# Conversion transfers on GpSimd's queue and fills from SBUF on SyncE's queue, in a fused attention, MoE and MLP kernel

## The chip, the cores and the metric

One of the cores of a Trainium2 chip runs the whole kernel. The metric is the device time of one execution in microseconds (us), the median of several runs. The engines are TensorE (PE in the profile), VectorE (DVE), ScalarE (ACT), GpSimd (POOL) and SyncE (SP), each with an instruction queue of its own; a DMA is issued by an instruction in such a queue and waits in it, in order, like any other.

## The reference

Three layers stand one behind the other; the output of each is the input of the next.

```python
# q, k, v: [4, 12, 448, 64]
scores = scale * np.matmul(q, k.transpose(0, 1, 3, 2))
scores = np.einsum('bhij,hg->bgij', scores, w_pre)      # heads mixed
scores = scores - np.max(scores, axis=-1, keepdims=True)
attn = np.exp(scores)
attn = attn / (np.sum(attn, axis=-1, keepdims=True) + 1e-09)
attn = np.einsum('bhij,hg->bgij', attn, w_post)         # heads mixed again
x = np.matmul(attn, v)                                  # -> 1792 tokens x 768
...
# mixture of 8 experts, the best one for each token
expert_idx = np.argmax(x @ w_gate, axis=1)
out[mask] = gate_w[mask, None] * (np.maximum(xe @ w1[e], 0.0) @ w2[e])
...
# MLP, 768 -> 2048 -> 768
h = x @ w_in
out = (h * np.cos(h)) @ w_out
```

All inputs are float32 but w_in and w_out of the MLP, which come as float64.

## The kernel before, in words

**The stages.** The attention runs from the start to about 490 us, the experts to about 795 us, the MLP to the end. The change lies in the attention and in what runs beside it.

**The attention** takes 16 chunks of a batch's query rows. For each chunk `score` (L292) multiplies heads with heads into S tiles in SBUF. A chunk falls into blocks of ten query rows (180 in all). `block(n)` (L520) handles one of them: `relay` (L309) has a DMA on SyncE copy ten rows x 12 heads of S, 210 KB, into an x tile of 120 partitions (6 of these tiles rotate); an m matmul (L527) mixes the heads; VectorE takes the maximum `nm` (L530); ScalarE the exponential `E` (L534); VectorE the sum's reciprocal `rs` (L537, L539) and the scaled mixing matrix `kr` (L542); the pa matmuls (L548) mix again and transpose; a copy (L551) puts the result into `AT`. An m and the four pa of a block show in the trace as 2 and 8 records. The heads of the next batch are loaded on SyncE as kn and qn (L200) and vn (L209) and transposed on TensorE (L222). The first batch's heads come as fk and fq (L251), which GpSimd copies into kn and qn (L262) and late (L270). When a chunk is done, the products with v (L355, L366, L414) give rows of tokens: `rows_out` (L417) collects a chunk's rows in the tile xr (one buffer) and stores them to `xs` in DRAM (L426).

**The fills.** Eleven stretches of 64 rows in `ys` (the DRAM buffer that the experts write and the MLP reads) are padding that no expert may write, and they need some finite contents. `fill[X]` (L1865) writes one of them behind each of the first eleven xs stores, from 64 of the rows that were just stored.

**The conversion** (`narrow64`, L1765) turns w_in and w_out into float32 copies `wi` and `wo` in DRAM that the MLP loads later. There are 64 pieces of 128 x 384 numbers. `piece` (L651) is a loop body of five steps: load 128 x 3072 bytes, 384 KB, into a tile W of 2 buffers (L1786); square on ACT (L1790, into sq); three bit operations on VectorE (L1796 to L1798, into a tile f of 2 buffers); store f, 192 KB (L1802).

**What sets the order.** `Plan` (L63) runs a list schedule when the kernel is built: each step of a task has an engine, a cost in us (and kilobytes for a transfer) and a rank; the earliest possible step is taken next, and the engine's queue gets instructions in that order. `dma(d)` is a cost on SyncE. The pieces run as background (`bg=True`): a step of theirs is put where it delays no step in front. So costs, and the engine that they stand on, change the order of every queue, and the order is fixed before the kernel runs.

**The hand-over.** `between` (L1807) starts the experts: the row gather `gather(0)` (L1269, an indirect DMA on GpSimd into xg), its transposes px on TensorE (L1277), and expert weights r loaded on SyncE (L1251, L1255).

Of the kernel before, what the change touches and what calls it, by code (L numbers as in the profile page):

```python
# [12 lines left out]
F32 = mybir.dt.float32  # L13
# [166 lines left out]
def attention(ctx, qctx, tc, q, k, v, w_pre, w_post, wg, xs, lg, ident, nb=4, side=None, route=None, fill=()):  # L180
# [3 lines left out]
    nc = tc.nc  # L184
# [179 lines left out]
    def moved(copy, out, in_, n):  # L364
        if copy:
            copy(out, in_)  # L366
        else:
            bal.copy(out, in_, n)
# [48 lines left out]
    def rows_out(X, half, pt, copy=None):  # L417
        b, c = chunks[X]
        i0, n, _ = CH[c]
        t0 = b * S + i0  # L420
        if half == 0:
            XRW[X] = wk.tile([120, 768], F32, tag="xr", name=f"xr{X}", bufs=1)
        xr = XRW[X]
        moved(copy, xr[:n, half * 384 : half * 384 + 384], pt[:n].rearrange("p a d -> p (a d)"), 384)
        if half == 1:
            nc.sync.dma_start(out=xs[t0 : t0 + n], in_=xr[:n])  # L426
            if X < len(fill):
                fill[X](xs[t0 : t0 + HR])

    def rows(X):  # L430
        for half in range(2):
            rows_out(X, half, rows_mm(X, half))
# [35 lines left out]
    with tc.manual_schedule(engines=START):  # L468
        spin(9)
        for j in range(H // 2 + 1):  # L470
# [20 lines left out]
            if j > 0:  # L491
                n = CH[0][1]
# [13 lines left out]
    def dve(d):  # L506
        return {"DVE": (d - 0.07, d)}

    def act(d):
        return {"ACT": (d - 0.07, d)}  # L510
# [4 lines left out]
    def dma(d):  # L515
        return {"SP": (d, d)}
# [76 lines left out]
    def products(X):  # L593
        n = CH[chunks[X][1]][1]
        b = chunks[X][0]
        ats = [("AT", k) for k in range(first_of[X], end_of[X] + 1)]
        px = []
        for half in range(2):
            yield dict(run=pe(0.02 * n + 0.02), tiling="col", onward=True, on=ats + [("V", b)], take=["q"] + (["xc"] if half == 0 else []), give=["AT"] if half else [], ends=[("av", X, half)])
            px.append(av_mm(X, half))  # L600
        for half in range(2):
            eng = yield dict(run=copying(3 * n), give=["q"], ends=[("xc", X)] if half else [])
            av_out(X, half, px[half], by[eng])
        for half in range(2):
            yield dict(run=pe(0.33), take=["q"] + (["xr"] if half == 0 else []))
            pt = rows_mm(X, half)
            eng = yield dict(run=copying(384), give=["q"])
            rows_out(X, half, pt, by[eng])

        yield dict(run={"none": (0.0, 3.0)}, give=["xr"])  # L610
# [38 lines left out]
        yield dict(run={"none": (0.0, 0.0)}, on=[("xcs", G_[-1])], give=["xc"])  # L649

    def piece(i, load, square, bits, store):  # L651
        yield dict(run=dma(0.58), kb=393, take=["W"])
        load(i)
        yield dict(run=act(0.56), take=["sq"])
        square(i)
        for d, op in zip((0.36, 0.56, 0.56), bits(i)):
            yield dict(run=dve(d), take=["f"] if d == 0.36 else [], give=["W", "sq"] if False else [])
            op()
        yield dict(run=dma(0.42), kb=197, give=["W", "sq"])
        store(i)  # L660
        yield dict(run={"none": (0.0, 0.0)}, give=["f"])

# [29 lines left out]
    if side is not None:  # L692
        count, *ops = side
        for i in range(count):
            plan.add(4 + i * 170 / count, piece(i, *ops), bg=True)
    with tc.manual_schedule(engines=START | {mybir.EngineType.SP}):
        plan.run()
    return SimpleNamespace(
        last=last, X=len(chunks) - 1, av_mm=av_mm, av_out=av_out, logits_mm=logits_mm, logits_out=logits_out, logit_tiles=logit_tiles,
        rows_mm=rows_mm, rows_out=rows_out, pq=pq,  # L700
    )

# [6 lines left out]
HR = 64  # L709
# [477 lines left out]
class Experts:  # L1187
# [69 lines left out]
    def load(self, s, anew=False):  # L1257

        for i in range(3):
            self.load1(s, i, anew)  # L1260
        for i in range(4):
            self.load2(s, i, anew)
# [502 lines left out]
def narrow64(ctx, tc, pairs):  # L1765

    nc = tc.nc
    V = nc.vector
    wk = ctx.enter_context(tc.tile_pool(name="f64", bufs=2))
    C = 384
    jobs = []
    for src, dst in pairs:
        n = src.shape[0] * src.shape[1] // P
        sv = src.bitcast(I32).rearrange("(p a) d -> p (a d)", p=P)
        dv = dst.rearrange("(p a) d -> p (a d)", p=P)
        for j in range(n // C):  # L1780
            jobs.append((sv[:, 2 * C * j : 2 * C * j + 2 * C], dv[:, C * j : C * j + C]))
    W, SQ, F = {}, {}, {}

    def load(i):
        W[i] = wk.tile([P, C, 2], I32, tag="W", name=f"W{i}")
        nc.sync.dma_start(out=W[i], in_=jobs[i][0].rearrange("p (n two) -> p n two", two=2))  # L1786

    def square(i):
        SQ[i] = wk.tile([P, C], F32, tag="sq", name=f"sq{i}")
        nc.scalar.activation(SQ[i], W[i][:, :, 1].bitcast(F32), AF.Copy, scale=2.0**-112)  # L1790

    def bits(i):
        w, sq = W.pop(i), SQ.pop(i)
        f = F[i] = wk.tile([P, C], I32, tag="f", name=f"f{i}")
        return (
            lambda: V.tensor_scalar(f, w[:, :, 0], 29, None, op0=ALU.logical_shift_right),  # L1796
            lambda: V.scalar_tensor_tensor(f, sq.bitcast(I32), 3, f, op0=ALU.logical_shift_left, op1=ALU.bitwise_or),
            lambda: V.scalar_tensor_tensor(f, w[:, :, 1], -0x80000000, f, op0=ALU.bitwise_and, op1=ALU.bitwise_or),  # L1798
        )

    def store(i):
        nc.sync.dma_start(out=jobs[i][1], in_=F.pop(i).bitcast(F32))  # L1802

    return len(jobs), load, square, bits, store


# [41 lines left out]
def kernel(ctx, tc, q, k, v, w_pre, w_post, w_gate, w1, w2, w_in, w_out, out):  # L1848
    nc = tc.nc
    glob = ctx.enter_context(tc.tile_pool(name="glob", bufs=1))  # L1850
    dram = ctx.enter_context(tc.tile_pool(name="dram", bufs=1, space=bass.MemoryType.DRAM))
    ys = dram.tile([NH * HR + NF * P, 768], F32, name="ys")
    xs = dram.tile([NT * P, 768], F32, name="xs")
# [8 lines left out]
    ro = Routing(cr, tc, glob, consts, lg)  # L1862
    fill = []
    for at in (*range(HSURE * HR, NH * HR, HR), *range(NH * HR + NSURE * P, NH * HR + NF * P, HR)):
        fill.append(lambda a, at=at: nc.gpsimd.dma_start(out=ys[at : at + HR], in_=a))  # L1865
    with ExitStack() as cm:
        with ExitStack() as c:
            with ExitStack() as cq:
# [129 lines left out]
```

## Time and profile before

| | us |
|---|---|
| median of 3 runs | 1283.37 (1282.93 to 1285.02) |
| profiled execution, its own time | 1286.4 |
| span of its records | 1284.6 |
| TensorE busy in the span | 1265.5 (99%) |
| VectorE busy | 987.1 (77%) |
| ScalarE busy | 755.4 (59%) |
| GpSimd busy | 88.5 (7%) |

The span runs from the first to the last record of one execution. Busy times leave out register, semaphore and DMA-issuing instructions. An engine with a share of 99% over the whole span is read best by its waits: how many there are, and what ended each. In a timeline, an x behind a row is the number of records merged into it, and the bracket is the time in which the engine stood idle ahead of it, with the instruction that released it. A queue's own rows (SPq for SyncE) give the time that an issue took.

### The profile page before, as it was taken

The numbers are of one execution on the slowest core, as the hardware profiler recorded it, in microseconds if no ns is written. First come the engines' busy times: TensorE is split into PE (matmuls) and PEld (weight loads), VectorE is DVE, ScalarE is ACT, GpSimd is POOL, SyncE is SP. The second block draws the span as 40 slices with busy tenths as digits, with TensorE's granted clock in tenths as the row PEclk, the third lists the DMA queues.
The fourth block names the chain that finished last, engine by engine and source line by source line (L and its number), as shares of the span: only waits on it lengthen the run. The fifth ranks groups of instructions, "written<-read, shape, count | busy, mean of one in ns | idle before, by whom it ended". The sixth has DMA issues, their size and how long they took to land.

```text
span 1284.6 us, 24332 instructions
## 1 busy us (share of the span) xinstructions
PE 1265.5 (99%) x8719; PEld 1026.9 (80%) x8719; DVE 987.1 (77%) x2382; ACT 755.4 (59%) x1422; POOL 88.5 (7%) x97
## 2 busy tenths in 40 slices
PE   9999999999999999999999999999999999999997
PEld 5777777777877787876667998898888888888886
DVE  7888888888878878986667998987666667766663
ACT  6566666666666656766667988665434434444432
POOL 3000000000000000210000110011000200001001
PEclk9999999999999999999999999999999999999999
DMA  7768757775766546599977944664333333234201
GB/s 201 229 201 216 246 195 220 220 241 181 219 224 220 181 157 237 215 358 343 379 261 263 358 147 159 198 207 162 98 124 123 128 118 120 78 104 139 77 26 52
DMA packets 149008, 244.90 MB, mean 191 GB/s; under 512 B 42240, under 2 KB 106176, under 8 KB 148704
## 3 DMA queue, kind: packets, MB, share of 16 engines
q1 hardware_dynamic: 142528, 217.90, 51.7%
q0 software_dynamic: 3936, 19.27, 4.6%
q10 hardware_dynamic: 2416, 6.10, 1.2%
q8 instruction: 71, 1.16, 0.4%
q14 instruction: 57, 0.47, 0.1%
HBM read 219.05 MB, written 31.85 MB: 195 GB/s over the span
## 4 chain that ended last, share of the span: by engine, by line
PE 57%; DMA 1%; ACT 0%; DVE 0%; issue 0%; POOLq 0%; POOL 0%; ACTq 0%
PE op L1667 18%; PE dh L1727 18%; PE yp L1471 8%; PE h L1355 6%; PE yp L1426 2%; PE h L1406 2%; PE ph L1454 1%; PE dpt L1590 1%; PE px L1277 1%; DMA xg<-xs,idh 1%; PE ph L1415 0%; PE px L1388 0%; DVE wl L1169 0%; ACT wh L1168 0%; POOLq L1952 0%
## 5 line engine op out<-in xcount | busy, mean ns | idle before, releaser
L548 PEld LDWEIGHTS pa<-kr,E 120*112 120x112 f32 (+1 forms) x1440 | 166.5, 177 | 46.2 <-issue 32.7
L1169 DVE TENSOR_TENSOR wl<-r,wh 128x768 fp32r<-128x768 f32 (+1 forms) x176 | 180.5, 1062 | 23.1 <-ACT wh L1168 21.7
L548 PE MATMUL pa<-kr,E 120*112 120x120 f32 (+1 forms) x1440 | 181.5, 269 | 2.1 <-DVE rs L537 1.0
L1168 ACT CAST wh<-r 128x768 fp32r<-128x768 f32 (+1 forms) x176 | 160.9, 928 | 34.3 <-PE h L1355 19.3
L527 PE MATMUL m<-x,kpre 120*120 120x448 f32 x360 | 159.1, 546 | 2.2 <-DMA x<-S 2.2
L1169 DVE TENSOR_TENSOR wil<-wi,wih 128x768 fp32r<-128x768 f32 x64 | 60.8, 953 | 129.9 <-ACT wih L1168 129.9
L1667 PE MATMUL op<-woh,gh 128*128 128x512 f32 x448 | 151.9, 339 | 0.9 <-ACT gh L1698 0.9
L1667 PE MATMUL op<-wol,gh 128*128 128x512 f32 x448 | 150.9, 337 | 0.0
L1667 PE MATMUL op<-woh,gl 128*128 128x512 f32 x448 | 150.4, 336 | 0.0
L1168 ACT CAST wih<-wi 128x768 fp32r<-128x768 f32 x64 | 53.6, 843 | 155.9 <-PE dh L1727 155.9
L534 ACT ACTIVATE E<-m,nm 120x448 f32<-120x448 f32 x180 | 114.3, 635 | 46.6 <-DVE nm L530 21.5
L530 DVE TENSOR_REDUCE nm<-m 120x1 f32<-120x448 f32 x180 | 111.0, 617 | 20.4 <-PE m L527 16.7
L1727 PE MATMUL dh<-dxh,wih 128*128 128x512 f32 (+1 forms) x384 | 109.7, 365 | 0.3 <-ACT dhs L1731 0.3
L1727 PE MATMUL dh<-dxl,wih 128*128 128x512 f32 (+1 forms) x384 | 109.0, 363 | 0.0
L1727 PE MATMUL dh<-dxh,wil 128*128 128x512 f32 (+1 forms) x384 | 108.3, 363 | 0.0
L1667 PEld LDWEIGHTS op<-woh,gh 128*128 128x128 f32 x448 | 84.9, 189 | 11.4 <-ACT gh L1698 1.1
L1667 PEld LDWEIGHTS op<-wol,gh 128*128 128x128 f32 x448 | 84.9, 190 | 9.8
L1667 PEld LDWEIGHTS op<-woh,gl 128*128 128x128 f32 x448 | 84.7, 189 | 9.2
L551 ACT COPY AT<-pa 112x480 f32<-112x480 f32 (+1 forms) x103 | 58.4, 567 | 45.6 <-PE pa L548 40.0
L1168 ACT CAST woh<-wo 128x768 fp32r<-128x768 f32 x64 | 53.2, 836 | 53.0 <-PE op L1667 52.3
L355 PEld LDWEIGHTS px<-AT,vn 112*64 112x64 f32 x1536 | 73.7, 137 | 8.1 <-issue 3.2
L1727 PEld LDWEIGHTS dh<-dxl,wih 128*128 128x128 f32 x384 | 69.3, 189 | 11.5
(350 smaller groups left out, 2448.7 us busy)
## 6 DMA issues: line engine op xcount, KB each, us to landing
r<-in_moe_w_dram SPq DMA_DIRECT2D x39, 1024.0 KB
r<-in_moe_w_dram SPq DMA_DIRECT2D x52, 768.0 KB
x<-S SPq DMA_DIRECT2D x172, 210.0 KB
wi<-wi SPq DMA_DIRECT2D x32, 768.0 KB
wo<-wo SPq DMA_DIRECT2D x32, 768.0 KB
p<-in_moe_w_dram SPq DMA_DIRECT2D x15, 1024.0 KB
p<-in_moe_w_dram SPq DMA_DIRECT2D x20, 768.0 KB
W<-in_moe_w_in_dram SPq DMA_DIRECT2D x32, 384.0 KB
```

The source lines that it names most:

```text
L355: nc.tensor.matmul(px[64 * e : 64 * e + 64, pr, :n], VN[b, g // 3][:, g % 3, cc], AT[X][:, cc, g, :n], start=(cc == 0), stop=(cc == 3))
L527: nc.tensor.matmul(ps[:M, :S], kpre[:M, :M], x[:M], start=True, stop=True)
L530: nc.vector.reduce_max(nm[:M], ps[:M, :S], axis=AX.X, negate=True)
L534: last["act"] = nc.scalar.activation(e[:M], ps[:M, :S], AF.Exp, bias=nm[:M], scale=1.0, accum_out=sg[:M])
L548: nc.tensor.matmul(pa[:112, c, :120], e[:M, c * 112 : c * 112 + 112], kr[:M], start=True, stop=True)
L551: last["post"] = by[eng](AT[X][:, :, :, j0 : j0 + m], pa[:112, :, :120].rearrange("p c (g i) -> p c g i", i=10)[:, :, :, :m])
L1168: self.latest["A"] = nc.scalar.copy(hi, src).ins
L1169: self.latest["V"] = nc.vector.tensor_tensor(lo, src, hi.bitcast(F32), op=ALU.subtract).ins
L1355: self.nc.tensor.matmul(hp[n], a[:, k], w[:, n * 512 : n * 512 + 512], start=(k == 0 and i == 0), stop=(k == 5 and i == 2))
L1471: self.nc.tensor.matmul(yp[n][:, :384], a[:, k], w[:, n * 384 : n * 384 + 384], start=(k == 0 and i == 0), stop=(k == 7 and i == 2))
L1667: nc.tensor.matmul(bank[:, to], g[:, u * P : u * P + P], w[:, of], start=first, stop=(f == 15 and i == 2), skip_group_check=(n == 1))
L1727: nc.tensor.matmul(hp[:, :N], w[:, k], x[:, k, :N], start=(k == 0 and i == 0), stop=(k == 5 and i == 2))
```

## The change

The conversion's loads (L1786) and stores (L1802) are issued on GpSimd in place of SyncE, and the planner counts 1.0 us of GpSimd for each in place of 0.58 and 0.42 us of SyncE. The fills (L1865) are issued on SyncE in place of GpSimd, and their source is 64 rows of xr in SBUF rather than the 64 rows of xs in DRAM, so they read what the store ahead of them reads and don't wait for it.

```diff
@@ rows_out
             nc.sync.dma_start(out=xs[t0 : t0 + n], in_=xr[:n])
             if X < len(fill):
-                fill[X](xs[t0 : t0 + HR])
+                fill[X](xr[:HR])
@@ piece
-        yield dict(run=dma(0.58), kb=393, take=["W"])
+        yield dict(run={"POOL": (1.0, 1.0)}, kb=393, take=["W"])
         load(i)
...
-        yield dict(run=dma(0.42), kb=197, give=["W", "sq"])
+        yield dict(run={"POOL": (1.0, 1.0)}, kb=197, give=["W", "sq"])
         store(i)
@@ narrow64
-        nc.sync.dma_start(out=W[i], in_=jobs[i][0].rearrange("p (n two) -> p n two", two=2))
+        nc.gpsimd.dma_start(out=W[i], in_=jobs[i][0].rearrange("p (n two) -> p n two", two=2))
...
-        nc.sync.dma_start(out=jobs[i][1], in_=F.pop(i).bitcast(F32))
+        nc.gpsimd.dma_start(out=jobs[i][1], in_=F.pop(i).bitcast(F32))
@@ the main kernel
-        fill.append(lambda a, at=at: nc.gpsimd.dma_start(out=ys[at : at + HR], in_=a))
+        fill.append(lambda a, at=at: nc.sync.dma_start(out=ys[at : at + HR], in_=a))
```

SyncE's queue has 1137 instructions before and 1020 with the change (128 leave, 11 come), GpSimd's 130 and 257. What stands in the queues at three places is shown below; a row is the line, the operation, what it writes and what it reads, with the program's buffer numbers.

SyncE in the first blocks of the attention, where x are the operands of the m matmuls, kn and qn the next batch's heads, W a piece's load; before:

```order
L309 DMA x6_561<-S0_275 120x1x448
L209 DMA vn0_2_569<-in_v_dram 112x3x256
L309 DMA x7_577<-S0_275 120x1x448
L200 DMA qn1_0_589<-in_q_dram 112x4x64 x2
L1786 DMA W0_607<-in_moe2_w_in_dram 128x768
L309 DMA x8_616<-S0_275 120x1x448
L309 DMA x9_628<-S0_275 120x1x448
L209 DMA vn0_3_641<-in_v_dram 112x3x256
L309 DMA x10_646<-S0_275 120x1x448
L309 DMA x11_663<-S0_275 120x1x448
L1786 DMA W1_672<-in_moe2_w_in_dram 128x768
L309 DMA x12_680<-S1_482 120x1x448
```

and with the change:

```order
L200 DMA qn1_0_563<-in_q_dram 112x4x64 x2
L309 DMA x6_578<-S0_275 120x1x448
L200 DMA kn1_1_585<-in_k_dram 112x4x64 x2
L209 DMA vn0_2_602<-in_v_dram 112x3x256
L309 DMA x7_611<-S0_275 120x1x448
L309 DMA x8_627<-S0_275 120x1x448
L309 DMA x9_643<-S0_275 120x1x448
L309 DMA x10_654<-S0_275 120x1x448
L309 DMA x11_672<-S0_275 120x1x448
L200 DMA qn1_1_677<-in_q_dram 112x4x64 x2
L209 DMA vn0_3_701<-in_v_dram 112x3x256
L309 DMA x12_708<-S1_486 120x1x448
```

W0 and W1 have left the queue, x7 to x11 stand closer together, and heads have taken some of the room.

GpSimd in the start, among the copies of the first batch's heads, before:

```order
L262 COPY kn0_2_297<-fk_193 112x2x4x64
L262 COPY qn0_2_299<-fq_194 112x2x2x64
L929 MEMSET edge_7630 128x56
L262 COPY kn0_3_327<-fk_193 112x2x4x64
L262 COPY qn0_3_329<-fq_194 112x2x2x64
L262 COPY kn0_4_357<-fk_193 112x2x4x64
```

and with the change:

```order
L262 COPY kn0_2_297<-fk_193 112x2x4x64
L262 COPY qn0_2_299<-fq_194 112x2x2x64
L1786 DMA W0_478<-in_moe2_w_in_dram 128x768
L1786 DMA W1_482<-in_moe2_w_in_dram 128x768
L262 COPY kn0_3_327<-fk_193 112x2x4x64
L262 COPY qn0_3_329<-fq_194 112x2x2x64
L929 MEMSET edge_7630 128x56
L262 COPY kn0_4_357<-fk_193 112x2x4x64
```

W0 and W1 stand between the copies of the third and of the fourth pair of heads. At the end of the attention GpSimd's queue has W63's load, the stores of f62 and f63, and then xg0, the first gather (L1269); before, eleven fills and nothing of the conversion stood ahead of xg0.

TensorE in the start, where s1_8 to s1_11 are scores of the second chunk and m0 the first block; before:

```order
L292 MATMUL s1_6_513<-KH0_3_347,QL0_3_352 120x448
L292 MATMUL s1_7_514<-KH0_3_347,QL0_3_352 120x448
L527 MATMUL m0_527<-x0_478,kpre_211 120x448
L527 MATMUL m1_536<-x1_480,kpre_211 120x448
L292 MATMUL s1_8_540<-KH0_4_380,QH0_4_384 120x448
L292 MATMUL s1_9_541<-KH0_4_380,QH0_4_384 120x448
L292 MATMUL s1_8_540<-KL0_4_381,QH0_4_384 120x448
```

and with the change:

```order
L292 MATMUL s1_10_541<-KH0_5_410,QH0_5_414 120x448
L292 MATMUL s1_11_542<-KH0_5_410,QH0_5_414 120x448
L292 MATMUL s1_10_541<-KL0_5_411,QH0_5_414 120x448
L292 MATMUL s1_11_542<-KL0_5_411,QH0_5_414 120x448
L292 MATMUL s1_10_541<-KH0_5_410,QL0_5_415 120x448
L292 MATMUL s1_11_542<-KH0_5_410,QL0_5_415 120x448
L527 MATMUL m0_557<-x0_480,kpre_211 120x448
L527 MATMUL m1_572<-x1_484,kpre_211 120x448
L527 MATMUL m2_581<-x2_503,kpre_211 120x448
L527 MATMUL m3_590<-x3_505,kpre_211 120x448
L527 MATMUL m4_600<-x4_525,kpre_211 120x448
L548 MATMUL pa0_614<-kr0_598,E0_574 112x120 x4
```

Before, m0 and m1 stand ahead of the twelve score matmuls of s1_8 to s1_11; with the change these twelve stand ahead of m0, and m0 to m4 follow each other.

## Rows read from the trace of the kernel before

**Rows 1.** Engines by stage: us, busy of PE, PEld, DVE, ACT, POOL; clock, DMA, GB/s
```profile
24.00:490.00 466.00, 461.55 (x4215) 355.36 (x4215) 391.41 (x1321) 288.77 (x709) 6.51 (x12) 1.00 0.68 210
...
10.00:12.00 2.00, 2.00 (x19) 1.38 (x19) 1.17 (x3) 1.78 (x5) 0.51 (x1) 1.00 1.22 224
```

**Rows 2.** TensorE's timeline in the first blocks: start us, us, engine, line, operation [idle before]
```profile
21.03 0.98 PE L527 MATMUL m<-x,kpre 120*120 120x448 f32 x2
23.28 0.98 PE L527 MATMUL m<-x,kpre 120*120 120x448 f32 x2 [1.27 <-DMA x<-S]
...
31.91 0.98 PE L548 MATMUL pa<-kr,E 120*112 120x120 f32 x8
32.73 0.92 PE L527 MATMUL m<-x,kpre 120*120 120x448 f32 x2
33.48 0.98 PE L548 MATMUL pa<-kr,E 120*112 120x120 f32 x8
35.41 0.98 PE L527 MATMUL m<-x,kpre 120*120 120x448 f32 x2 [0.94 <-DMA x<-S]
```

**Rows 3.** TensorE's timeline at its four later waits
```profile
106.42 0.38 PE L222 MATMUL tp<-ident,qn 112*128 112x112 f32 x2 [1.08 <-DMA qn<-in_q_dram]
...
134.40 0.33 PE L548 MATMUL pa<-kr,E 108*112 108x120 f32 x1 [0.62 <-ACT E L534]
...
249.75 0.43 PE L548 MATMUL pa<-kr,E 120*112 120x120 f32 x2 [0.96 <-DVE rs L537]
...
354.05 0.57 PE L222 MATMUL tp<-ident,kn 112*128 112x112 f32 x4 [0.29 <-DMA kn<-in_k_dram]
```

**Rows 4.** SyncE's queue in the timeline: issues at 33, 98 and 128 us
```profile
33.35 0.52 SPq L1786 DMA_DIRECT2D W<-in_moe_w_in_dram  x1
...
98.01 0.57 SPq L1786 DMA_DIRECT2D W<-in_moe_w_in_dram  x1
...
99.63 1.27 SPq L200 DMA_DIRECT2D qn<-in_q_dram  x2
...
127.92 0.42 SPq L1786 DMA_DIRECT2D W<-in_moe_w_in_dram  x1
```

**Rows 5.** Who waited for whom, whole span: total us, times, longest us
```profile
ACT sq L1790 <- DMA W<-in_moe_w_in_dram: 22.2, 14, 4.9
...
SPq L1802 <- DVE f L1798: 36.8, 24, 4.1
```

**Rows 6.** ScalarE's timeline at one of its waits for a W
```profile
133.10 0.56 ACT L1790 ACTIVATE sq<-W 128x384 f32<-128x384 f32 x1 [1.58 <-DMA W<-in_moe_w_in_dram]
```

**Rows 7.** Two lines' DMAs on GpSimd: issue ns min/median/max; us to landing min/median/max
```profile
L1865 POOL DMA_DIRECT2D ys<-xs x11: 486/486/539, 65.3 to 374.6; - x11
...
DMA to landing us min/median/max: 3.1/4.3/6.2
...
L1269 POOL DMA_INDIRECT xg<-xs,ids x13: 944/955/1914, 452.5 to 728.4; - x13
...
DMA to landing us min/median/max: 3.8/6.9/14.3
```

**Rows 8.** GpSimd's timeline at three places, and VectorE's beside the last
```profile
7.62 0.40 POOL L262 COPY qn<-fq 112x256 f32<-112x256 f32 x1
...
12.45 0.40 POOL L262 COPY qn<-fq 112x256 f32<-112x256 f32 x1 [0.35 <-DMA fq<-in_q_dram]
...
539.24 9.67 POOL L1269 DMA_INDIRECT xg<-xs,idh  x1 [6.91 <-PE px L1388]
...
541.98 6.16 DVE L1169 TENSOR_TENSOR wl<-r,wh 128x768 fp32r<-128x768 f32 x7
```

**Rows 9.** The end of the attention: TensorE's first px, VectorE's nm before the last conversion operation
```profile
490.52 0.71 PE L1277 MATMUL px<-ident,xg 128*128 128x128 f32 x5
...
481.31 0.62 DVE L530 TENSOR_REDUCE nm<-m 120x1 f32<-120x448 f32 x1
```

## Prediction

> **What bounds the kernel now.** I read four views, in this order: engines by stage, TensorE's timeline at the start, who waited for whom, and the timelines of the two queues that the change touches. The stage that holds nearly all of the change is the attention, 24 to 490 us. There TensorE is busy 461.55 of 466.00 us at a granted clock of 1.00, while VectorE has 391.41, ScalarE 288.77 and GpSimd 6.51 us [rows 1]. So the stage ends when TensorE has got through its list, and only two things can move the time: TensorE's few waits, and work that is added to its list (none is). The stages behind it run in an unchanged order and are not touched, apart from the hand-over at 490 us.
>
> TensorE's waits are small and can be counted. In the start, the second m (L527) waits for its x tile: it starts at 23.28, the first at 21.03 [rows 2]. An m that has its operand gives way to its successor after 0.75 us (32.73 to 33.48), though it is drawn 0.92 to 0.98 long; so the true wait there is 23.28 - 21.03 - 0.75 = 1.50 us, where the bracket says 1.27. Likewise a pa (L548) takes 0.82 us start to start (31.91 to 32.73) and is drawn 0.98: each bracket is about 0.16 short. After 24 us there are five waits worth naming: 0.94 at 35.41 for an x tile [rows 2], and 1.08, 0.62, 0.96 and 0.29 at 106.42, 134.40, 249.75 and 354.05 [rows 3]. Together 3.89 us by the brackets, 3.89 + 5 x 0.16 = 4.7 us true.
>
> What they have in common is SyncE's queue. At 33.35 it issues a conversion load W for 0.52 us, and only behind it the x tiles that the m at 35.41 and its successors want; at 98.01 another W (0.57 us) stands ahead of the q heads issued at 99.63 that TensorE awaits until 106.42 [rows 4]. The queue also stood 36.8 us in 24 waits for f (L1802), with x tiles and heads queued behind [rows 5]. The waits at 134.40 and 249.75 come by ScalarE: it sits 1.58 us at 133.10 for a W [rows 6] that was issued at 127.92 [rows 4], then the exponential comes late.
>
> **The change part by part.** *Taken off SyncE:* 64 loads and 64 stores, with their 36.8 us of waiting. The x tiles and heads then go out earlier; the five waits become 0 at best. Bounds 0 to -4.7; I take -4.7, since an issue that stands ahead is 0.5 us or more and the waits are of that size.
>
> *Put on GpSimd:* 128 issues. The trace has no plain load of this size on that queue. The nearest rows are the fills (L1865), 0.486 to 0.539 us, and the row gathers (L1269), median 0.955 us [rows 7]: 128 x 0.49 = 63 to 128 x 0.955 = 122 us, on an engine with 6.51 us of work in the stage's 466. That is 13 to 26% of it: hidden, 0 us. Its cover is that one piece comes every 450 / 64 = 7.0 us and needs two issues. A store that waits for f now holds up the next loads on GpSimd instead, but the next load but one needs the same tile W to come free, by the same L1798, so little is lost.
>
> *Waits that may appear.* Before, ScalarE waited 14 times for a W (22.2 us) [rows 5] and two of these reached TensorE. The loads' way to landing may be no shorter from GpSimd (fills land in a median of 4.3 us [rows 7]). I take one new wait of the mean size, 3.89 / 5 = 0.78, rounded to +0.7; bounds 0 and +3.9 (as many new as old).
>
> *Order on TensorE at the start.* Before, m0 and m1 run, then twelve score matmuls, then m2; now the twelve run ahead of m0. They take the place in which TensorE waited for x1, since x1 lands by 23.28 while the list is busy: -1.5 us (all but none of the 1.50). The five m that follow in a row are 0.75 us apart, which the x tiles, one issue each, about follow.
>
> *Two loads at the start.* W0 and W1 now stand on GpSimd behind the copy at 7.62 [rows 8] and wait for nothing, so 2 x 384 KB go out from 8 us on, when first heads are still on their way: at 10 to 12 us the DMA share is 1.22 at 224 GB/s [rows 1]. 786 KB at 224 GB/s is 3.5 us; bounds 0 (they fill gaps) to +3.5 (all of it reaches TensorE). I take the middle, +1.8: the queues share the engines, so at most about half of their time should go to the new loads, and GpSimd's copy of the heads at 12.45 [rows 8] already waits for its data, so that such a delay shows. The two issues also push back GpSimd's own copies by 1 to 1.9 us.
>
> *The fills:* 11 move to SyncE, 0.49 us each there, read SBUF and need no wait for the xs store. 11 x 0.5 = 5.4 us on a queue that lost 128 issues; 0 us. On GpSimd they would have to wait up to 48.8 us for the store ahead of them with conversions queued behind, so this part is a condition of the first and brings nothing alone.
>
> *The first gather.* L1269 now stands behind the last two stores of the conversion. The last L1798 comes just behind the nm that now runs at 481.31 [rows 9], so f63 is ready at 482.5, its store is issued by 483.5, the gather by 484.6. It landed in 3.8 to 6.9 us (minimum and median [rows 7]): 488.4 to 491.5, and TensorE wants it at 490.52 [rows 9]. So 0 to +1.0, with a slow issue (1.914 in place of 0.955) to +1.9; I take +0.4.
>
> Sum: -4.7 - 1.5 + 1.8 + 0.7 + 0.4 = -3.3 us. The profiled execution lasted 1286.4 us (span 1284.6), the median of the runs is 1283.37; it lies 3.0 above them and is not one of the three, so the difference is applied to both: 1283.37 - 3.3 = **1280.1 us** (profiled: 1283.1).
>
> **The rivals.** *Nothing is lost anywhere:* no start shift, no new wait, no late gather: -6.2, 1277.2 us. For it: the DMA engines' share is 0.68 in the stage [rows 1].
>
> *The gain is eaten at both ends:* start shift at its bound and the gather late by 1.5: -4.7 - 1.5 + 3.5 + 0.7 + 1.5 = -0.5, 1282.9 us. For it: the share of 1.22 at 10 us; against: the early heads were issued before the W.
>
> *The waits only move:* the x tiles and heads land no earlier, because their transfers, not their issue, are late. Then the term of -4.7 is 0 and that for new waits too: -1.5 + 1.8 + 0.4 = +0.7, 1284.1 us. For it: the q heads of 99.63 landed 6.8 us later, and at most 0.6 of this was the W's issue [rows 4]. The Trainium skill speaks for this rival ("DMA: Bandwidth & Descriptors", Issuing engines are not separate DMA queues): transfers started by any engine run on the same 16 DMA engines, and spreading them saves only issue time. By that rule alone the gain is no more than the issue time that stands in front of a late tile, about 0.5 us each or 2.5 in all, which would give 1282.3; no run here tests it yet.
>
> *Slower: GpSimd's issues are held up by VectorE.* One gather issue took 9.67 us at 539.24, in the middle of back-to-back L1169 operations on VectorE (seven of them, 6.16 us, from 541.98 [rows 8]), against a median of 0.955 [rows 7]. VectorE is 84% busy in the attention. If issues stretch beyond 3.5 us on the mean, two of them no longer fit into a piece's 7.0 us, W comes late, and each late W costs TensorE 0.78 + 0.16 us as at 134.40 and 249.75; every fifth of 64 is 13 x 0.94 = +12.2, less the 3.3: 1292.3 us. Against it: the 11 fills, spread over the same attention with the same VectorE work, all took 0.486 to 0.539 us [rows 7]. The Trainium skill has the rule behind such a case ("SBUF — State Buffer", SBUF: two separate sides): GpSimd writes the descriptors of its DMAs itself and cannot while VectorE runs an operation in a two-port mode. The fills' rows don't show it in this stage; the gather's row does look like it.
>
> **How the numbers follow.** Chances: the forecast 0.48; nothing lost 0.14; eaten at both ends 0.18; the waits only move 0.12; GpSimd held up 0.08. What a measurement of this kernel can tell from no change is 0.2%, 2.6 us: faster is below 1280.8, slower above 1285.9. Of the forecast's 0.48 I count 0.36 as faster and 0.12 as same; with 0.14 that is 0.50 faster. Same: 0.12 + 0.16 + 0.10 = 0.38. Slower: 0.08 + 0.02 + 0.02 = 0.12. The range goes from 1276.7 (nothing lost, less half a microsecond, as low as a run shown lies under the median) to 1284.6 (the waits only move, plus the same); left out are the last rival and the tails, 0.2.
>
> **What would show it.** Right: on TensorE in 24 to 490 us less than 1.5 us of waits in brackets, no wait for x at the second m, L1786 on GpSimd at 0.5 to 1.1 us each, and the stage's end, the first px (L1277), 3 to 4 us ahead of 490.52. Start contention: heads' copies on GpSimd later than 12.45 by over a microsecond, and the first m later than 22.4. The gather: a wait for xg ahead of L1277. GpSimd held up: L1786 and L1802 issues of several microseconds beside VectorE's work, and ScalarE's waits for W above 22.2 us. I am wrong if TensorE has lost its waits and the span has not become shorter: then its list has grown elsewhere, by order alone.

## The result, and the profile after

The changed kernel is slower. Its median is 1294.17 us against 1283.15 us for the kernel before in the same set of runs: a ratio of 1.008, with a 95% interval of 1.0067 to 1.0092, so +11 us where -3.3 was forecast. In a second set of runs (a1_again, below) it is 1295.85 us, ratio 1.0085 (1.0065 to 1.0105). The changed kernel's eight runs in the two sets go from 1291.3 to 1298.2 us, the 21 of the kernel before in the second set from 1281.5 to 1288.2: they don't overlap.

Where does it go? The page of the changed kernel gives TensorE nearly the same busy time as before, 1265.9 us, in a span that is 5.5 us longer (its profiled execution, 1291.8 us, is one of its fastest); GpSimd has 152.8 us.

```profile
span 1290.1 us, 24392 instructions
...
PE 1265.9 (98%) x8719; PEld 1026.2 (80%) x8719; DVE 985.3 (76%) x2379; ACT 756.8 (59%) x1425; POOL 152.8 (12%) x214
```

So the list is not longer; TensorE waits more. The waits of TensorE in 24 to 500 us, changed kernel (waiter, what it waited for: total us, times, longest us):

```profile
PE m L527 <- DMA x<-S: 6.8, 6, 2.8
PE tp L222 <- DMA qn<-in_q_dram: 2.0, 3, 1.2
PE tp L222 <- DMA kn<-in_k_dram: 0.9, 1, 0.9
```

Before, the same three stood at 0.9, 1.1 and 0.3 us [rows 2, 3]; the two waits that came by ScalarE and VectorE (134.40 and 249.75 us) are gone. Data that comes by SyncE's queue is what is late now. TensorE's timeline shows the largest wait, at 44.94 us:

```profile
34.83 0.98 PE L527 MATMUL m<-x,kpre 120*120 120x448 f32 x2 [1.23 <-DMA x<-S]
...
41.12 0.98 PE L548 MATMUL pa<-kr,E 120*112 120x120 f32 x8
44.94 1.85 PE L527 MATMUL m<-x,kpre 120*120 120x448 f32 x2 [2.83 <-DMA x<-S]
```

The m at 44.94 multiplies x12 (block 12's tile), which SyncE issued at 36.05, behind two loads of heads and one of v. On GpSimd's queue two conversion loads went out together half a microsecond earlier. SyncE's timeline, then GpSimd's:

```profile
33.70 1.52 SPq L200 DMA_DIRECT2D qn<-in_q_dram  x2
35.26 0.61 SPq L209 DMA_DIRECT2D vn<-in_v_dram  x1
36.05 11.54 SPq L309 DMA_DIRECT2D x<-S  x7
```

```profile
34.98 0.54 POOL L1802 DMA_DIRECT2D wi<-f  x1 [5.41 <-DVE f L1798]
35.51 1.08 POOL L1786 DMA_DIRECT2D W<-in_moe_w_in_dram  x2
```

Before, x12 was issued at 34.05, and one load, W1, had gone out ahead of it [rows 4]:

```profile
34.05 0.81 SPq L309 DMA_DIRECT2D x<-S  x1
```

The engines by stretch (columns as in [rows 1]) show what the wait costs beyond its length; the last row is the kernel before in the last of these stretches:

```profile
36.00:40.00 4.00, 4.00 (x26) 2.82 (x25) 3.80 (x11) 1.73 (x5) 0.59 (x2) 1.00 1.10 284
40.00:44.00 4.00, 2.10 (x16) 1.52 (x14) 2.95 (x11) 1.89 (x6) 0.00 (x0) 1.00 0.72 237
44.00:48.00 4.00, 3.06 (x10) 1.58 (x12) 1.11 (x5) 0.46 (x1) 0.00 (x0) 0.60 0.65 224
```

```profile
44.00:48.00 4.00, 4.00 (x26) 2.86 (x25) 3.86 (x12) 1.65 (x5) 0.00 (x0) 1.00 0.78 268
```

In the changed kernel, from 36 to 40 us the DMA engines are full (1.10, 284 GB/s); from 40 to 44 TensorE is busy 2.10 of 4 us; from 44 to 48 its granted clock is 0.60, a mix of 2.4 and 1.2 GHz (before: 1.00 and no wait), and the m there is drawn 1.85 us rather than 0.98.

How long do x tiles take to land? The trace's DMA records tell: x tiles are its only packets of 1792 bytes, 21,504 of them in each trace read here, one for each partition of a tile. Counted in order of their ends against the issues, tile k has landed when as many have ended as tiles 0 to k have rows. Microseconds from issue to landing:

```
kernel                               median   90%    over 6 us (of 180)
before                                3.26    4.89     4
e3  fills only                        3.28    4.69     5
e8  first two loads on GpSimd         3.30    4.82     1
e2  new order, all on SyncE           3.50    4.91     2
e10 stores on GpSimd                  3.55    5.32     9
e9  loads on GpSimd                   4.22    6.30    23
e1  old order, all on GpSimd          4.27    5.64    14
e4  as changed, heads late            4.32    6.00    17
e6  as e1, first loads at 27 us       4.36    6.40    21
changed kernel                        4.39    5.92    16
e5  as changed, pieces late           4.46    5.96    17
e7  as e1, loads twice                6.05    8.30    91
```

x12 took 6.8 us before and 7.6 after the change. It was issued 2.0 us later, so it landed 2.8 us later: most of this wait, the largest, comes from SyncE's order and not from a slower transfer.

To say where the rest is, I compare the start of the same block's m in the two traces. Block 13 starts 4.35 us later than before (49.71 against 45.36), block 114 2.7 us (321.36 against 318.66), block 138 6.45 us (383.62 against 377.17), the last one 6.2 us (492.41 against 486.17). Another count, the "excess" below, takes for each matmul its start less the start of the one before, less the median of that difference for the same pair of lines, and sums what is 0.06 us or more. By it the changed kernel has about 5.5 us more than the kernel before in 25 to 50 us and 4 to 5 us more in 325 to 400. Two places, then, carry the loss.

### The profile page after: what moved, and what is told of

Same layout as the page of the kernel before. It is cut to its first block, busy times and chain, and to the rows that moved or that the text cites. A ratio compares the mean times of both kernels' runs of the same rounds, so it can differ in the third digit from the quotient of the medians.

```text
span 1290.1 us, 24392 instructions
## 1 busy us (share of the span) xinstructions
PE 1265.9 (98%) x8719; PEld 1026.2 (80%) x8719; DVE 985.3 (76%) x2379; ACT 756.8 (59%) x1425; POOL 152.8 (12%) x214
## 4 chain that ended last, share of the span: by engine, by line
PE 57%; DMA 0%; ACT 0%; DVE 0%; issue 0%; POOLq 0%; POOL 0%; ACTq 0%
PE op L1667 18%; PE dh L1727 18%; PE yp L1471 8%; PE h L1355 6%; PE yp L1426 2%; PE h L1406 2%; PE ph L1454 1%; PE dpt L1590 1%; PE px L1277 1%; DMA xg<-xs,idh 0%; PE ph L1415 0%; PE px L1388 0%; DVE wl L1169 0%; POOLq L1952 0%; ACT wh L1168 0%
## 5 line engine op out<-in xcount | busy, mean ns | idle before, releaser
L527 PEld LDWEIGHTS m<-x,kpre 120*120 120x120 f32 x360 | 55.0, 184 | 30.2 <-issue 18.6
```

The costliest lines, as they stand in the source:

```text
L527: nc.tensor.matmul(ps[:M, :S], kpre[:M, :M], x[:M], start=True, stop=True)
```

## The experiments

Two theories. **Order:** with the conversion off SyncE's account, the planner puts heads in front of x tiles and pieces earlier; SyncE's and GpSimd's traffic piles up. **Sharing:** transfers in a second queue take turns with the x tiles on the DMA engines, and the tiles land later, whatever the order.

**e1_old_plan** undoes the costs, so every engine but GpSimd keeps the old order.

```diff
-        yield dict(run={"POOL": (1.0, 1.0)}, kb=393, take=["W"])
+        yield dict(run=dma(0.58), kb=393, take=["W"])
...
-        yield dict(run={"POOL": (1.0, 1.0)}, kb=197, give=["W", "sq"])
+        yield dict(run=dma(0.42), kb=197, give=["W", "sq"])
```

> The changed kernel, but the planner still counts the conversion's load and store as 0.58 and 0.42 us of SyncE, so that TensorE, VectorE, ScalarE and SyncE keep the order of the kernel before (SyncE without the 128 transfers, with the 11 fills); the transfers are issued on GpSimd. Theory 1 (the loss is SyncE's new order: the planner, with the conversion off SyncE's account, puts heads in front of x tiles; x12 is issued at 36.05 in place of 34.05): the loss of 11 us goes, 1279 to 1284 us, and no wait for x above 1 us. Theory 2 (the loss is that GpSimd's packets share the DMA engines with the x tiles, which take 4.39 in place of 3.26 us to land, median): the loss stays, 1289 to 1295 us, with the x tiles' median still above 4 us.

1285.08 us, ratio 1.001 (1.0001 to 1.0019), 1.1 us above the range for order. The loss is all but gone, though x tiles land nearly as late as in the changed kernel (4.27 us): order decides whether sharing hurts. But nothing is gained either, with 128 issues off SyncE.

**e2_old_queue** keeps the new order and issues the transfers on SyncE again (`nc.sync` at L1786 and L1802).

> The changed kernel's planner costs and so its order, but the conversion's loads and stores are issued on SyncE at the places that this order gives them (W0 and W1 stand ahead of x0 and x1 there). Theory 1 (order): as slow as the changed kernel or slower, 1290 to 1300 us, since SyncE has the new order and the conversion's issues too. Theory 2 (shared DMA engines): near the kernel before, 1283 to 1287 us, x tiles landing in about 3.3 us (median).

1289.88 us, ratio 1.0048 (1.0034 to 1.0062): between the two forecasts. The new order without GpSimd's queue costs about half, and SyncE's own issues of the conversion, at places planned for another queue, are in that half. The x tiles' median is 3.50 us, and TensorE's excess in 25 to 50 us is less than 1 us above that of the kernel before (some 5.5 in the changed kernel). As the queue in the old order costs 0.9 us (e1), the other half needs GpSimd's queue and the new order together.

**e3_fill_only** changes the fills alone in the kernel before.

```diff
-                fill[X](xs[t0 : t0 + HR])
+                fill[X](xr[:HR])
...
-        fill.append(lambda a, at=at: nc.gpsimd.dma_start(out=ys[at : at + HR], in_=a))
+        fill.append(lambda a, at=at: nc.sync.dma_start(out=ys[at : at + HR], in_=a))
```

> The kernel before with only the fills changed: on SyncE, from the rows in SBUF, behind the xs store. Eleven issues of 0.5 us on SyncE. Both theories: within 0.2% of before, 1282 to 1285 us. If it is slower by several us, the fills' transfers on SyncE's queue (192 KB each ahead of x tiles) are a cause of their own.

1285.5 us, ratio 1.0012 (0.9998 to 1.0025): not told apart from no change, and no large cause (at most 3 us by the interval).

**a1_again** is the changed kernel once more.

> The changed kernel once more, for a second profile: its runs went from 1291.8 to 1295.0 us and the profiled one was the fastest. Theory 1 and 2 alike: about 1293 us; the waits for x between 30 and 50 us and between 345 and 385 us come again, and the granted clock of 0.60 in 44 to 48 us too, perhaps lower or longer; what varies among runs is expected there and not behind 500 us.

Much as expected, with a median 3 us higher. This profiled execution took 1298.2 us. Its wait for x12 is 4.14 us, and the clock is low for longer:

```profile
40.00:44.00 4.00, 1.20 (x10) 0.94 (x8) 2.08 (x8) 1.02 (x4) 0.00 (x0) 1.00 0.81 199
44.00:48.00 4.00, 2.65 (x6) 1.26 (x8) 0.77 (x3) 0.05 (x1) 0.00 (x0) 0.57 0.66 193
48.00:52.00 4.00, 4.00 (x20) 3.07 (x17) 2.39 (x10) 2.02 (x5) 0.00 (x0) 0.57 0.43 126
```

6.65 us busy at 0.57 is work for 3.8 us at full clock: an estimate of 2.9 us lost to the clock, on top of the wait. In 340 to 400 us the mean granted clock is 0.97 in this execution, against 1.00 in the first. So these two executions differ in how long a wait becomes and how far the clock falls after it: one source of the spread among runs.

**e4_heads_late** and **e5_pieces_late** part the planner's doing in the start. e4 lets a head's load (in `heads`) be placed only behind an x tile's landing, e5 a piece's load:

```diff
+        late = {(1, 0, 0): 1, (1, 0, 1): 4, (1, 1, 0): 9, (1, 1, 1): 11, (3, 5, 0): 126, (3, 5, 1): 126}.get((b, j, s_), 14)
-        yield dict(run=dma(1.36), kb=230, take=[tag])
+        yield dict(run=dma(1.36), kb=230, take=[tag], on=[("x", late)])
```

```diff
+        late = {0: 4, 1: 8, 2: 15, 3: 17, 4: 20, 5: 20}.get(i, 22)
-        yield dict(run={"POOL": (1.0, 1.0)}, kb=393, take=["W"])
+        yield dict(run={"POOL": (1.0, 1.0)}, kb=393, take=["W"], on=[("x", late)])
```

> The changed kernel, but the planner may place the next batch's first heads only behind about the x tiles behind which they stood before (kn1_1 behind x12, qn1_1 behind x14), while the conversion's pieces start as early as in the changed kernel. If heads in front of x tiles are the cause of the start's loss (excess of TensorE's pitch of 7.8 to 9.0 us in 25 to 50 us, against 2.3 before): 1288 to 1290 us, the wait for x12 gone. If the early pieces are (W2 and W3 together at 35.5 us): still 1293 to 1296 us, with the wait at about 45 us.

1291.51 us, ratio 1.007 (1.005 to 1.009), with runs from 1288.0 to 1295.8: between the two forecasts, and by the intervals not told apart from the changed kernel. In the profiled run, the fastest, the wait for x12 is gone. W2 and W3 still go out together, at 33.92. So what the heads alone cost stays undecided.

> The changed kernel, but the planner may place the first six loads of the conversion only where they stood before (W0 behind x4's landing, W1 x8, W2 x15 and so on); by itself this puts the heads back behind x12 and x14 too, and the two scores' place on TensorE. W0 and W1 are still issued at 8 us. If what the planner did in the start is the cause of the start's loss: 1287 to 1290 us, with what is left in 340 to 390 us (about 4 us more than before). If the issue of W0 and W1 at 8 us is: still over 1292 us.

1287.66 us, ratio 1.0034 (1.0021 to 1.0048), in the range for the planner's start. Holding back the first pieces in the planner, with the heads that follow them back behind x tiles, removes some 7 us of the 11, and the runs lie within 3 us again. In 24 to 50 us no matmul of the profiled run waits any more; W2 and W3 go out when the pile of heads is past (GpSimd's timeline; this kernel's lines stand one further down):

```profile
45.09 0.54 POOL L1803 DMA_DIRECT2D wi<-f  x1 [5.80 <-DVE rs L539]
45.62 1.07 POOL L1787 DMA_DIRECT2D W<-in_moe_w_in_dram  x2
```

**e6_old_plan_held** is e1 with W0 and W1 held until the blocks have begun, about when they were issued before.

```diff
+        if i < 2:
+            nc.gpsimd.tensor_copy(W[i][:1, 0, :1], HOLD["kr"][:1, :1].bitcast(I32))
         nc.gpsimd.dma_start(out=W[i], in_=jobs[i][0].rearrange("p (n two) -> p n two", two=2))
```

> e1_old_plan (the planner's costs of before, transfers on GpSimd), but W0 and W1 wait on GpSimd for a scaled mixing matrix of the first blocks (one element of it is copied into the tile first), so they are issued at about 27 and 32 us rather than at 8. If their early issue cost e1_old_plan its waits between 12 and 24 us and with them the granted clock of 0.56 to 0.59 in 24 to 28 us: 1.5 to 3 us faster than e1_old_plan, 1282 to 1283.5 us, clock 1.00 there. If not: 1285 us as e1_old_plan.

The expectation fell: 1287.82 us, ratio 1.0029 (1.0017 to 1.004), some 2.5 us slower than e1 by the two ratios. The clock did stay at 1.00, but the loads now lie beside x tiles. GpSimd's issues, then TensorE's waits (the lines stand up to four further down):

```profile
27.50 0.61 POOL L1790 DMA_DIRECT2D W<-in_moe_w_in_dram  x1 [0.30 <-POOL W L1789]
...
32.78 0.56 POOL L1790 DMA_DIRECT2D W<-in_moe_w_in_dram  x1 [0.30 <-POOL W L1789]
```

```profile
34.85 0.98 PE L528 MATMUL m<-x,kpre 120*120 120x448 f32 x2 [1.07 <-DMA x<-S]
38.52 1.01 PE L528 MATMUL m<-x,kpre 120*120 120x448 f32 x2 [0.29 <-DMA x<-S]
40.71 0.98 PE L528 MATMUL m<-x,kpre 120*120 120x448 f32 x2 [1.18 <-DMA x<-S]
```

The x tiles issued from 29 to 36 us took 6.1 to 8.5 us to land. This run is the nearest to the bare exchange of the queue: order and time of the first loads as before, and 4.0 us slower (the fills' part, which e3 puts between 0 and 0.25%, is in it). On GpSimd, the loads at 8 us were cheaper than the loads at 27 and 33.

**e7_loads_twice** doubles the suspected traffic: each load of e1 goes out a second time.

```diff
+        D = wk.tile([P, C, 2], I32, tag="D", name=f"D{i}", bufs=1)
+        nc.gpsimd.dma_start(out=D, in_=jobs[i][0].rearrange("p (n two) -> p n two", two=2))
```

> e1_old_plan with every conversion load issued a second time on GpSimd, into one more tile that nobody reads: 25 MB more on GpSimd's queue, SyncE's and the computing engines' order unchanged. If x tiles land later because GpSimd's transfers share the DMA engines with them (median 3.26 us before, 4.27 in e1_old_plan, 4.36 in e6_old_plan_held): about 5 us or more in the median, and waits for x and heads that make it 5 to 15 us slower, 1290 to 1300 us. If that sharing is harmless: within 2 us of e1_old_plan, 1283 to 1287 us.

1328.02 us, ratio 1.0346 (1.0331 to 1.036), more than expected. The direction is that of sharing (6.05 us to land; the waits for x alone are 11.8 us in 13 times), but the size is not a clean price: the second load waits for the one tile D, 147.0 us in all on GpSimd, and already in the start 6.5 us of a copy that TensorE awaits are lost behind it.

**e8_first_two, e9_loads_only, e10_stores_only, e11_first_two_stores** take the kernel before, with its planner and its fills, and move one part each to GpSimd: W0 and W1; all loads; all stores; all stores with W0 and W1.

```diff
-        nc.sync.dma_start(out=W[i], in_=jobs[i][0].rearrange("p (n two) -> p n two", two=2))
+        (nc.gpsimd if i < 2 else nc.sync).dma_start(out=W[i], in_=jobs[i][0].rearrange("p (n two) -> p n two", two=2))
```

> The kernel before with only the conversion's first two loads (W0, W1) issued on GpSimd, where they go out at 8 us; the other 62 loads, all stores and the fills as before, the planner too. SyncE loses its issues at 28.46 and 33.35 and 768 KB leave the stretch of 28 to 36 us, in which x tiles take 5 to 7 us to land. If the traffic beside the x tiles is what counts, the early loads cost little (e1_old_plan issues them at 8 us and was 2.7 us faster than e6_old_plan_held): the wait of 1.1 us at 35.41 goes, 1281.5 to 1283.5 us. If the loads at 8 us hold up the first heads by more than that: 1284 to 1286 us.

1282.81 us, ratio 0.9995 (0.9981 to 1.0009): in the median no measurable gain. Yet in the profiled run, 1281.19 us and the fastest of five, not only the wait at 35.41 is gone but all five that the prediction counted; no wait of TensorE from 24 to 500 us is above 0.3 us.

```diff
-        nc.sync.dma_start(out=W[i], in_=jobs[i][0].rearrange("p (n two) -> p n two", two=2))
+        nc.gpsimd.dma_start(out=W[i], in_=jobs[i][0].rearrange("p (n two) -> p n two", two=2))
```

> The kernel before with only the conversion's 64 loads issued on GpSimd; stores on SyncE, fills and planner as before, so every other queue keeps its order. SyncE is rid of 64 issues but x tiles share the engines with loads in a second queue. If the sharing with the loads is the queue's price: x tiles land in about 4 us (median, 3.26 before), time 1284 to 1288 us. If taking issues off SyncE gains what the prediction said: 1279 to 1282 us.

1307.12 us, ratio 1.0193 (1.0175 to 1.0211): far outside both. The x tiles land at 4.22 us, but the loss has another source. The fills are still on GpSimd and wait there for the xs store (53.4 us in 5 times; the profile puts the other fills' waits down to other releasers, as below), and now loads stand behind them. GpSimd, ScalarE and TensorE near 138 us, where the xs store was issued at 126.8 and the fill behind it at 130.19:

```profile
130.19 0.51 POOL L1865 DMA_DIRECT2D ys<-xs  x1 [12.71 <-DVE nm L530]
130.73 1.09 POOL L1786 DMA_DIRECT2D W<-in_moe_w_in_dram  x2
```

```profile
137.36 0.55 ACT L1790 ACTIVATE sq<-W 128x384 f32<-128x384 f32 x1 [4.88 <-DMA W<-in_moe_w_in_dram]
```

```profile
138.59 0.71 PE L548 MATMUL pa<-kr,E 108*112 108x120 f32 x2 [3.69 <-ACT E L534]
```

Two loads leave right behind the fill, ScalarE waits 4.88 us for the first, and TensorE 3.69 us for ScalarE's exponential. With the fills on SyncE and the same order, all transfers on GpSimd cost 0.9 us (e1). So the second part of the change, the fills, is what makes the first part possible, as the prediction had it; this run doesn't price the loads' queue.

```diff
-        nc.sync.dma_start(out=jobs[i][1], in_=F.pop(i).bitcast(F32))
+        nc.gpsimd.dma_start(out=jobs[i][1], in_=F.pop(i).bitcast(F32))
```

> The kernel before with only the conversion's 64 stores issued on GpSimd; loads on SyncE, fills and planner as before. SyncE is rid of 64 issues and of its 36.8 us of waiting for f; the second queue carries half the bytes of the loads (192 KB a piece). If waiting for f in SyncE's queue was what made x tiles late: waits at 106, 134 and 250 us go, 1280 to 1282 us. If those waits cost nothing: 1282 to 1285 us, x tiles landing in 3.3 to 3.7 us.

1283.39 us, ratio 1.0 (0.9991 to 1.0009). No store of SyncE waits for f any more, and nothing is gained: the 36.8 us of [rows 5] cost no time that can be measured. In the profiled run the waits at 106, 134 and 250 us are gone, but TensorE waits 2.4 us in three times for x tiles, 0.9 us in one before. And SyncE now stands before the x tiles themselves: an x tile's copy can't be issued until an m has read what its buffer held before. Before, then in e10, then in the changed kernel:

```profile
SPq L309 <- PE m L527: 37.0, 63, 1.8
```

```profile
SPq L309 <- PE m L527: 63.4, 70, 3.2
```

```profile
SPq L309 <- PE m L527: 88.2, 74, 5.0
```

The last takes the edits of e8 and e10 together.

> The kernel before with all stores and the first two loads of the conversion on GpSimd, the 62 other loads on SyncE; fills and planner as before. If e8_first_two's change at the start and the stores' part add up: 1279.5 to 1282.5 us, faster than both kernels. If they don't, 1282 to 1285 us as e8_first_two.

1283.0 us, ratio 0.9993 (0.9983 to 1.0004). The parts don't add up to a gain that can be measured; no version tried here beats the kernel before beyond doubt.

## Why the prediction was wrong, step by step

The forecast was -3.3 us and +11.0 came, 14.3 us apart. e1 keeps every term but the one for TensorE's order: without it the prediction's sum is -1.8 us, and e1 measured +0.9, so 2.7 us of the miss hang on those terms. The other 11.6 come with the new order, put at -1.5 and measured at some +10 (the changed kernel less e1); by e2, about half of that only together with GpSimd's queue.

**The step that failed first is the term of -4.7 us**, "the x tiles and heads then go out earlier; the five waits become 0". It failed in three ways. First, SyncE's freed time did not go into earlier issues alone: its waits for a buffer of x to come free grew from 37.0 to 88.2 us, so how early a tile goes out is set by TensorE's own pace too. Second, a transfer in a second queue runs beside the tiles instead of in front of some of them: 3.26 us to land became 4.27 to 4.46 in every kernel with all of the conversion on GpSimd once, and the three waits for SyncE's data went from 2.3 to 9.7 us. The bare exchange (e6) measured +4.0, fills included, where this term, with the loads out of SyncE's way, had -4.7. Third, the 4.7 us were counted in one execution, which lasted 3.0 us longer than the median, and taken off the median as if that had them too. e8's profiled run has none of these waits and took 1281.19 us; the medians of the kernel before, 1283.2 to 1284.2 in the sets above, are 2 to 3 us over that. By this estimate, from one execution of each kernel, hardly more than these 2 to 3 us were there to gain.

The rival "the waits only move" named the right resource, but gave the sharing no price: I had bounded it by "no gain". The Trainium skill's sentence cited there ("DMA: Bandwidth & Descriptors", Issuing engines are not separate DMA queues), that transfers of all engines interleave on the same 16 DMA engines, agrees with these landings; that the tiles pay 1.1 us for it in the median is this case's number.

**The planner's order was priced at one place only.** This is the larger part of the miss. The -1.5 us for TensorE's order in the start is borne out for a moment: the m that waited 1.50 us is gone, the first one waits 0.44, and block 3's m starts 2.1 us earlier than before (25.13 against 27.26), where 0.8 us is a pa that now stands behind it. The m of that row run 0.9 us apart, not 0.75, and by block 8 the lead is lost again. The same excerpt showed heads moved ahead of x7 and x12 on SyncE, and I gave them no term. On SyncE a piece's load competed with relays, and the planner's background rule let the relays pass; on GpSimd nothing competes, so a load is placed as soon as its tile is free, and the pieces start earlier (f0's store goes out at 29.02 us; in e1, with the old order, at 40.19). W2 and W3, two loads of heads and one of v then meet x12 to x17 on full DMA engines. Undoing this start, pieces and heads together (e5), returns some 7 of the 11 us.

**The upper bound of the new waits was no bound.** "As many new as old", +3.9, came from a trace in which the tiles landed in 3.3 us. TensorE's waits answer to the margin between a tile's landing and its use, and when 1.1 us is taken off the margins the old count says nothing. Nor did the new waits come by the way that the term looked at: ScalarE waits for no W any more in the changed kernel's attention (22.2 us before). Behind the longest wait the granted clock fell to 0.57 to 0.60 for 4 to 8 us, which no term held at all.

**The two loads at 8 us** were put at +1.8. In e1's profiled run a cost of that size is there: blocks 4 to 7 start 2.0 us later than before, behind waits for heads' copies and x tiles and a granted clock of 0.57, after a stretch with TensorE busy 2.41 of 4 us:

```profile
24.00:28.00 4.00, 4.00 (x15) 2.21 (x14) 2.29 (x7) 2.32 (x6) 0.00 (x0) 0.57 0.80 220
```

By block 13 only 0.4 us of it is left, since the wait at 35.41 is gone. So the loads at 8 us are a gain against the same loads at 27 and 33 us (e6 less e1, some 2.5 us), and in the kernel before they cost nothing that can be measured (e8). In the changed kernel TensorE waits 0.7 us for GpSimd's copies.

**Right:** TensorE bounds the attention, the rest of the program runs as before, GpSimd's issues cost nothing in themselves (below), the fills had to leave GpSimd (e9), and the late first gather, put at +0.4, costs about nothing: the last store goes out at 489.60, xg at 490.79, and the first px runs at 496.75 without a wait for it. That px is the sum of the attention: 6.2 us later than in [rows 9], in one of the fastest executions. The changed kernel's two lines on GpSimd, issue durations in ns and landings in us:

```profile
L1786 POOL DMA_DIRECT2D W<-in_moe_w_in_dram x32: 536/538/718, 8.4 to 246.6; - x32
...
DMA to landing us min/median/max: 3.3/5.2/9.6
```

```profile
L1802 POOL DMA_DIRECT2D wi<-f x32: 542/544/549, 29.0 to 260.6; - x32
...
DMA to landing us min/median/max: 2.1/3.4/6.0
```

So the rival that gave nearly the right time, GpSimd held up by VectorE at 1292.3 us, came near it by luck, and is refuted by its own sign: it needed issues above 3.5 us on the mean, and the longest of the 128 was 0.718. The rule of the Trainium skill cited with it ("SBUF — State Buffer", SBUF: two separate sides) isn't seen at work in these 64 loads and 64 stores.

**What stays open.** The 4 to 5 us of excess in 325 to 400 us: heads 1.2 and 0.9 us late at 345 and 352, x tiles 1.0 us late at 379 and 382. e2 has excess there with the new order and no GpSimd queue (some 2 us), e1 hardly any with the sharing alone; the two together were not taken apart. And e5 still stands some 3 us above e1 with nearly the same start.

## What to carry to other kernels

A transfer that leaves a busy queue for an idle one doesn't leave the DMA engines: before pricing the issue time that it frees, look at how long the transfers of the bound engine's operands take to land, and at the margin that they have; here 1.1 us of landing time stood against a gain of 4.7 us on paper. Before taking waits off a time, ask whether they were counted in an execution of that time; here the profiled one was 3.0 us slower than the median. In a planned kernel, a cost that moves to an engine without competitors also takes away what kept a background step back, so read what moved on the other queues and give each of these moves a term. And a queue's waiting time that goes away may come back as another wait in the same queue (36.8 us here, worth nothing that could be measured, while waits for free buffers grew).

## What the runs showed of the hardware

The same load, 128 rows of 3072 bytes, shows in the trace as packets of 3072 bytes when SyncE issues it and as packets of 6144 bytes (0.234 us each in the median, against 0.074 for the x tiles' 1792 bytes) when GpSimd does. If a tile took turns packet by packet with such a load, it would wait three times its own time at each turn (an estimate from these two medians); whether this, rather than the mere number of bytes, is what the tiles pay was not tried. An issue of such a load took 0.54 us on GpSimd and 0.49 on SyncE in the median, so GpSimd's issues were not slow here.
